# A gated mix of an S4 convolution and linear attention: the issue order written out instead of planned at build time

## The chip, the cores and the metric

The kernel runs on one core of a Trainium2 chip. It uses five engines, each of which works through its own queue of instructions in order: TensorE (PE; its weight loads are listed apart as PEld), VectorE (DVE), ScalarE (ACT), GpSimd (POOL) and SyncE (SP), which issues nearly all DMAs. The metric is the device time of one launch in microseconds, the median of several runs.

## The reference

The inputs are u of shape [1, 2048, 512] in bf16, the parameters of a state space model (128 states for each of 512 channels), the weights of a linear attention with 32 heads of 16, and a gate vector. The output mixes two branches that read the same u:

```python
x = A_u
g = _sigmoid((x * gate_w).sum(-1, keepdims=True))
a = _A_ref(x, A_A_re, A_A_im, A_B_re, A_B_im, A_C_re, A_C_im, A_log_dt, A_Dskip)
b = _B_ref(x, B_wqkv, B_w_phi, B_wo)
return g * a + (1 - g) * b
```

Branch a builds a kernel K of length 2048 for each channel and convolves u with it by an FFT of length 4096; it then adds u times Dskip:

```python
logdA = dt * A
dB = dt * Bc
P = jnp.exp(logdA[:, :, None] * l[None, None, :])
K = jnp.einsum("dn,dnl,dn->dl", Cc, P, dB).real
...
Yf = Uf * Kf[None, :, :, :]
```

Branch b applies a softmax of the projection and one of its negative to queries and keys, and normalises:

```python
phi_q = jnp.concatenate([_softmax(pq, axis=-1), _softmax(-pq, axis=-1)], axis=-1)
phi_k = jnp.concatenate([_softmax(pk, axis=-1), _softmax(-pk, axis=-1)], axis=-1)
kv = jnp.einsum("bhsf,bhsd->bhfd", phi_k, v)
z  = jnp.einsum("bhsf->bhf", phi_k)
num = jnp.einsum("bhqf,bhfd->bhqd", phi_q, kv)
den = jnp.einsum("bhqf,bhf->bhq", phi_q, z)[..., None] + 1e-6
```

num / den goes through the output projection wo.

## The kernel before

The whole program is recorded before any instruction is issued. The class `Plan` (L92) holds 1009 nodes. A node is a short piece of work of one engine: a group of matmuls into one PSUM tile, one activation, one or a few VectorE operations, a few DMA issues. `add` (L112) gives it an engine, a cost estimate, the nodes that it depends on, and the buffers that it takes and drops. `run` issues the nodes one after the other, and since each engine's queue is worked in order, the order of the nodes is the order on every engine. Waits between engines follow from the tiles that the nodes read and write.

Buffers come in rings: two each of Ek and vr (exponentials and scaled values of a key block), A and R (the factors of the convolution kernel), XA, XK and bs, four of E and cs, one of KD and XUs. PSUM has rings too: `ps` (2), `p0` (2, until the polar stage ends), `bk` (3 banks, for keys, values, queries, aexp and bps), and `pf` (2, in place of bk once the queries are done). `prepare` (L146) turns a full ring into a dependency: the third A waits for the reader of the first.

Before the change, `schedule` (L161) makes the order at build time. It simulates the engines with the cost estimates and a latency LAT of 0.2 between engines, and takes next, of the nodes that could start earliest, the one with the longest chain of work behind it; a table TIES of seeds and amplitudes adds random numbers to these priorities. It also decides for each of 53 PSUM evictions (`evict`, L650 ff.) whether ACT (L662) or DVE (L660) does it, and which PSUM ring a tile comes from.

The work goes through these stages, in order of time:

- Prologue: loads (L1423 to L1437; UD is u laid out for the FFT, sixteen DMAs), trigonometric tables by DVE (`tgv`, L397/L398) and ACT, their parts TB (L414) and TJ (L428), small constants of the attention (L302 to L329), transposes of u (xps, L595).
- Polar stage: the state space parameters in polar form (L455 to L590, from `dtc`, the step size), and the spectrum of u: psA (L681) and psB (L293) on PE, cast to XAu and XU by ACT or DVE.
- Keys: for eight pairs of blocks of 128 positions, pk (L803), exp to Ek (ACT), its sums Zk (DVE, L815), a logarithm and an exponential on ACT, values vp (L835), scaling to vr (DVE, L839) and the product kvp (L848).
- KV: the state is arranged (L919 to L931), multiplied with wo (mps, L955) and cast to Mw.
- Queries: four rounds of pq (L981), Eq = exp (ACT), sums zs (L996/L1000), lnZ, den and apm (L1012 to L1021), the factor aexp (L1041), Eq times aexp (DVE, L1046), the product bps (L1056) and its cast bs (ACT, L1066). Beside them runs the making of K: PE makes args (L876/L894), ACT takes exponentials E and sines and cosines cs; between the two kinds it loads another table (L75). DVE multiplies tables into A (three operations a half, L1102 to L1104) and E with cs into R (two operations, L1116/L1117, and a negation, L1114). PE contracts them (kps, L280, two chunks for each pair), ACT casts to KD (L1135), PE transforms (psA, L1147), ACT casts to XA (L1153).
- Convolution: the rest of the making of K, and psB (L1206), XK (ACT, L1214), t = XU times XK (DVE, L1221/L1222), psz (L1244), Zr, a round trip through memory (L1254, L1263), psy (L1301/L1307), the gated sum bS (DVE, L1328) and the stores (L1336).
- Tail: the last transforms and stores (L1276 to L1336).

Of the kernel before, what the change touches and what calls it, by code (L numbers as in the profile page):

```python
# [91 lines left out]
class Plan:  # L92


    LAT = 0.2
    SLACK = 0.0
    TIES = ((52116, 4, 0.1), (24065, 0.5, 0.1), (41416, 1, 0.1), (45222, 1, 0.05), (61293, 2, 0.02), (71070, 0.5, 0.1),
# [48 lines left out]
    def prepare(self):  # L146
# [11 lines left out]
        for n in reversed(self.nodes):  # L158
            n.prio = n.cost + max([u.prio + self.LAT * (u.eng != n.eng) for u in n.users], default=0.0)

    def schedule(self, bias, slack=0.0):  # L161

        free, taken = {}, {r: 0 for r in self.k}
        given = {r: {} for r in self.k}
        shut, state, since, order = set(self.shut), None, {}, []
        for n in self.nodes:
            n.t, n.ring, n.open, n.ready = None, None, len(n.deps), 0.0
        left = [n for n in self.nodes if not n.open]
        while left:
            cand = []  # L170
            for n in left:
                best_e = None
                for e, c in (n.eng if isinstance(n.eng, list) else [(n.eng, n.cost)]):
                    t = free.get(e, 0.0) if e not in "WX" else 0.0
                    for d in n.deps:
                        x = d.end + (self.LAT if d.at != e else 0.0)
                        if x > t:
                            t = x
                    if best_e is None or t + c < best_e[0]:
                        best_e = (t + c, t, e, c)  # L180
                _, t, e, c = best_e
                if n.tab is not None and n.tab != state:
                    continue
                ok, ring = True, None
                for r in n.take:
                    if isinstance(r, str) and r not in self.dyn:
                        continue
                    alt = []
                    for q in ([r] if isinstance(r, str) else r):
                        m = taken[q] - self.k[q]  # L190
                        if q in shut or (m >= 0 and m not in given[q]):
                            continue
                        alt.append((max(t, given[q][m].end + self.LAT if m >= 0 else since[q].end if q in since else 0.0), -self.k[q] + taken[q], q))
# [1365 lines left out]
```

## Time and profile before

| | before |
|---|---|
| median of 3 runs | 340.84 us (338.55 to 341.11) |
| span of the profiled execution | 340.1 us |
| mean granted TensorE clock | 0.836 |
| DVE busy | 279.3 us (82%), 478 instructions |
| ACT busy | 257.2 us (76%), 332 instructions |
| PE busy | 249.9 us (73%), 4320 matmuls |
| POOL busy | 12.2 us |
| DMA | 24.6 MB, 72 GB/s over the span |

The profile is of one execution, whose span is that of the first to the last instruction. A view by windows gives each engine's busy time in a stretch of the span; a view of waits gives, by engine and line, how long it stood idle and whose result ended that. Matmuls are pipelined, so a busy PE is not one at its peak.

### The profile page before, as it was taken

The numbers are of one execution on the slowest core, as the hardware profiler recorded it, in microseconds if no ns is written. First come the engines' busy times: TensorE is split into PE (matmuls) and PEld (weight loads), VectorE is DVE, ScalarE is ACT, GpSimd is POOL, SyncE is SP. The second block draws the span as 40 slices with busy tenths as digits, with TensorE's granted clock in tenths as the row PEclk, the third lists the DMA queues.
The fourth block names the chain that finished last, engine by engine and source line by source line (L and its number), as shares of the span: only waits on it lengthen the run. The fifth ranks groups of instructions, "written<-read, shape, count | busy, mean of one in ns | idle before, by whom it ended". The sixth has DMA issues, their size and how long they took to land.

```text
span 340.1 us, 9815 instructions
## 1 busy us (share of the span) xinstructions
PE 249.9 (73%) x4320; PEld 145.7 (43%) x4320; DVE 279.3 (82%) x478; ACT 257.2 (76%) x332; POOL 12.2 (4%) x24
## 2 busy tenths in 40 slices
PE   0416665469998979569999998976776769878860
PEld 0405554355554424233644544534343433456630
DVE  8968999995897985997598896399999999994531
ACT  2847998896978557965976897899979998888200
POOL 5420010000000000000000000000000000000000
PEclk9956569576999978957999999996997995797775
DMA  9991600000000000001111011281177178768444
GB/s 138 253 152 34 153 3 0 2 0 2 2 3 2 4 0 2 2 1 29 37 24 26 17 33 31 48 222 45 64 185 148 60 179 192 187 174 173 113 77 81
DMA packets 58665, 24.62 MB, mean 72 GB/s; under 512 B 54144, under 2 KB 55296, under 8 KB 58112
## 3 DMA queue, kind: packets, MB, share of 16 engines
q1 hardware_dynamic: 54400, 23.10, 31.1%
q10 hardware_dynamic: 4224, 0.92, 1.9%
q8 instruction: 33, 0.54, 0.7%
q14 instruction: 8, 0.07, 0.1%
HBM read 11.42 MB, written 8.39 MB: 58 GB/s over the span
## 4 chain that ended last, share of the span: by engine, by line
DVE 40%; PE 37%; ACT 7%; issue 6%; DMA 4%; SPq 3%; ACTq 1%; DVEq 0%
PE bps L1056 7%; DVE R L1117 5%; DVE A L1104 5%; DVE Atmp L1103 5%; DVE A L1102 5%; PE pk L803 5%; PE vp L835 4%; PE pq L981 3%; PE args L876 3%; SPq L1428 3%; DVE R L1116 3%; DMA Cim<-in_A_C_im_dram 2%; PE kps L280 2%; PE aexp L1041 2%; PE psz L1276 2%
## 5 line engine op out<-in xcount | busy, mean ns | idle before, releaser
L83 ACT ACTIVATE E<-args 128x1024 bf16<-128x1024 f32 x32 | 32.1, 1039 | 3.7 <-PE args L876 3.6
L1056 PE MATMUL bps<-Mw,Eq 128*128 128x512 bf16 x128 | 31.9, 394 | 1.1 <-DVE Eq L1046 1.1
L83 ACT ACTIVATE cs<-args 128x1024 bf16<-128x1024 f32 x32 | 30.8, 1034 | 0.1
L1046 DVE TENSOR_TENSOR Eq<-Eq,aexp 128x512 bf16<-128x512 bf16 x32 | 20.4, 682 | 10.2 <-PE aexp L1041 10.2
L681 PE MATMUL psA<-W,UD 128*64 128x256 bf16 x128 | 15.6, 396 | 16.8 <-DMA ldc<-in_A_log_dt_dram 5.7
L75 ACT ACT_TABLE_LOAD x20 | 25.7, 1283 | 1.1 <-PEq L1543 0.7
L1116 DVE TENSOR_TENSOR R<-E,cs 128x1024 bf16<-128x1024 bf16 x32 | 21.9, 685 | 4.4 <-PE kps L280 4.4
L876 PE MATMUL args<-selE,stat 64*128 64x512 bf16 x64 | 21.3, 446 | 5.1 <-ACT cs L83 2.9
L280 PE MATMUL kps<-R,A 128*32 128x64 bf16 x1024 | 18.9, 230 | 8.2 <-DVE A L1104 3.8
L815 DVE TENSOR_REDUCE Zk<-Ek 128x64 f32<-128x1024 bf16 x16 | 18.8, 1214 | 6.0 <-ACT Ek L83 5.8
L1104 DVE TENSOR_TENSOR A<-A,Atmp 128x1024 bf16<-128x1024 bf16 x32 | 22.1, 692 | 1.1
L1102 DVE TENSOR_TENSOR A<-Ctab,Dtab 128x1024 bf16<-128x1024 bf16 x32 | 21.9, 685 | 1.2 <-PE kps L280 1.2
L83 ACT ACTIVATE Ek<-pk 128x512 bf16<-128x512 f32 x32 | 16.7, 603 | 7.9 <-PE pk L803 7.9
L280 PEld LDWEIGHTS <-A 128*32 128x32 bf16 x1024 | 17.2, 152 | 12.0 <-issue 7.1
L1103 DVE TENSOR_TENSOR Atmp<-Ctab,Dtab 128x1024 bf16<-128x1024 bf16 x32 | 21.9, 684 | 0.0
L595 PE MATMUL xps<-ident,UD 128*128 128x128 bf16 x64 | 7.5, 296 | 18.9 <-DVE tgv L397 10.4
L1244 PE MATMUL psz<-t,TI 128*128 128x512 bf16 x56 | 18.2, 457 | 4.2 <-ACT cs L83 3.0
L681 PEld LDWEIGHTS <-UD 128*64 128x64 bf16 x128 | 12.2, 205 | 20.1 <-issue 19.8
L839 DVE TENSOR_TENSOR vr<-vp,vr 128x512 bf16<-128x512 f32 x32 | 19.6, 682 | 0.0
L83 ACT ACTIVATE Eq<-pq 128x512 bf16<-128x512 f32 x32 | 16.8, 614 | 3.3 <-PE pq L981 3.3
L1056 PEld LDWEIGHTS <-Eq 128*128 128x128 bf16 x128 | 12.0, 101 | 16.9 <-DVE Eq L1046 3.0
L1214 ACT CAST XK<-psB 128x1024 bf16<-128x1024 f32 x16 | 16.1, 1027 | 1.5 <-PE psB L1206 1.0
(195 smaller groups left out, 564.4 us busy)
## 6 DMA issues: line engine op xcount, KB each, us to landing
XUs<-XU SPq DMA_DIRECT2D x8, 512.0 KB, 6.6
Zd<-Zr SPq DMA_DIRECT2D x14, 256.0 KB, 4.8
ZT<-Zd SPq DMA_DIRECT2D x6, 512.0 KB, 5.5
UD<-in_A_u_dram SPq DMA_DIRECT2D x16, 128.0 KB, 5.4
bSd<-bs SPq DMA_DIRECT2D x16, 128.0 KB, 1.9
bS<-bSd SPq DMA_DIRECT2D x4, 512.0 KB, 7.9
out_dram<-bS SPq DMA_DIRECT2D x30, 64.0 KB, 2.3
wqk<-in_B_wqkv_dram SPq DMA_DIRECT2D x1, 1024.0 KB, 6.4
```

The lines of the kernel that those rows point to most:

```text
L75: p = self.nc.scalar.preload_act_table_set(name)
L83: i = self.nc.scalar.activation(**kw)
L280: nc.tensor.matmul(kps[32 * dj:32 * dj + 32, g4, e, :], lhsT=A[:, ri, :, :, d].rearrange("p a b -> p (a b)"), rhs=R[:, ri, d, :], start=(r ...
L681: nc.tensor.matmul(box.ps[64 * e:64 * e + 64, i, :], lhsT=g.UD[:].rearrange("p t (e g) -> p g e t", e=2)[:, gw * h + 4 * g4 + i, e, :], rh ...
L839: nc.vector.tensor_tensor(out=K.v[:, u, sg, :, 0:32].rearrange("p m (h e) -> p m h e", e=16), in0=box.ps[:].rearrange("p (m h e) -> p m h ...
L876: nc.tensor.matmul(box.ps[:, 8 * j:8 * j + 8, :], lhsT=g.stat[0:64, G, :], rhs=g.selE[0:64, d0:d0 + 8, :], start=True, stop=True, tile_pos ...
L1046: nc.vector.tensor_tensor(out=e, in0=e, in1=box.ps[:], op=ALU.mult)
L1056: nc.tensor.matmul(box.ps[:], lhsT=Q.e[:, m, sg, 128 * i:128 * i + 128], rhs=g.Mw[:, 4 * sg + m, :], start=(k == 0), stop=False, skip_grou ...
L1102: nc.vector.tensor_tensor(out=c.A[:, o], in0=Cb(i0), in1=Db(j0), op=ALU.mult)
L1103: nc.vector.tensor_tensor(out=tmp[:], in0=Cb(i1), in1=Db(j1), op=ALU.mult)
L1104: nc.vector.tensor_tensor(out=c.A[:, o], in0=c.A[:, o], in1=tmp[:], op=op)
L1116: nc.vector.tensor_tensor(out=c.R[:, o, :, 32:64], in0=E[:, :, 32:64], in1=x, op=ALU.mult)
```

## The change

The planner is gone. The class holds a string ORDER with the 1009 node numbers in the order in which they are issued, two digits to the base 64 each; SIDES, one digit for each of the 53 evictions (0 is ACT, 1 is DVE); and RINGS, one for each PSUM tile that has a choice of rings. `run` asserts that every node comes after those it depends on. Nodes, tiles, rings and operations are those of before; 15 evictions go to DVE and 38 to ACT, as before, but not all the same ones. The tables tell a reader nothing and are cut.

```diff
-    LAT = 0.2
-    SLACK = 0.0
-    TIES = ((52116, 4, 0.1), (24065, 0.5, 0.1), (41416, 1, 0.1), (45222, 1, 0.05), (61293, 2, 0.02), (71070, 0.5, 0.1),
...
+    DIGITS = "0123456789abcdefghijklmnopqrstuvwxyzABCDEFGHIJKLMNOPQRSTUVWXYZ-_"
+    ORDER = ("000f0g0h0b0c2u01040C0k0y0l0m0D0E0z0i0A0B0907050d02060F0a2o0n0j0p0q0e0r0t0u2v0o0G0s0v2s082p030H2t2q2r2k2l0w0I0J2F2G0K0M"
...
+    SIDES = ("00000000001010101000101010000000100100010011000010110")
...
-        for n in reversed(self.nodes):
-            n.prio = n.cost + max([u.prio + self.LAT * (u.eng != n.eng) for u in n.users], default=0.0)
-
-    def schedule(self, bias, slack=0.0):
...
-    def run(self):
-        self.tail = {}
+    def run(self):
+        code = {d: i for i, d in enumerate(self.DIGITS)}
+        order = [64 * code[a] + code[b] for a, b in zip(self.ORDER[0::2], self.ORDER[1::2])]
+        assert sorted(order) == list(range(len(self.nodes)))
+        names, sides, rings = [r for r in self.k if r in self.dyn], iter(self.SIDES), iter(self.RINGS)
+        for n in self.nodes:
+            n.at = n.eng[int(next(sides))][0] if isinstance(n.eng, list) else n.eng
+            n.ring = names[int(next(rings))] if n.dyn else None
         self.prepare()
-        T, order = self.schedule(self.bias(self.TIES), self.SLACK)
-        assert order is not None, "no piece can start"
-        for n in order:
+        done = set()
+        for i in order:
+            n = self.nodes[i]
+            assert all(d.i in done for d in n.deps)
+            done.add(i)
             self.cur = n
             n.fn()
-        return T
```

Three places show what moves. Lines of the new kernel are 70 lower than the same lines before (L590 is L660, L976 is L1046).

The first is DVE in the prologue. Before (tgv are the arguments of the trigonometric tables, TB and TJ two of these tables, the last row is the first of the attention's constants):

```order
L397 TENSOR_SCALAR tgv_161<-tgc,one 128x1024
L398 TENSOR_SCALAR tgv_161<-tgv_161 128x1024
L414 TENSOR_SCALAR TB<-TB 128x32x64
L397 TENSOR_SCALAR tgv_162<-tgc,one 128x1024
L398 TENSOR_SCALAR tgv_162<-tgv_162 128x1024
L428 TENSOR_SCALAR TJ<-tj 128x1024
L302 TENSOR_SCALAR mask_295<-c_293,if_h_140 128x8
```

And after (XAu is the cast of psA, the first stage of u's spectrum; pt is the first operation of the polar stage):

```order
L327 TENSOR_SCALAR tgv_157<-tgc,one 128x1024
L328 TENSOR_SCALAR tgv_157<-tgv_157 128x1024
L590 CAST XAu<-psA 128x256x4
L327 TENSOR_SCALAR tgv_158<-tgc,one 128x1024
L328 TENSOR_SCALAR tgv_158<-tgv_158 128x1024
L358 TENSOR_SCALAR TJ<-tj 128x1024
L344 TENSOR_SCALAR TB<-TB 128x32x64
L358 TENSOR_SCALAR TJ<-tj 128x1024
L590 CAST XAu<-psA 128x256x4 x2
L385 SCALAR_TENSOR_TENSOR pt_355<-Are,dtc 128x512
```

A cast of psA has come between the two pairs of trigonometric steps, and two more ahead of the polar stage; the attention's constants have moved behind it. On SP, the sixteen loads of UD, which psA reads, stand together in the new order; before, the five loads of weights (wc, gw, Dcol_b, wqk, Wv) stood between the first four and the other twelve.

The second place is ACT from the last key block to the first queries. Before (Zk and vr end a key block, Eq is the exponential of a query, Mw the attention's state with wo, cs the sines and cosines, E the exponentials, lnZ opens a query round):

```order
L83 ACTIVATE Zk<-Zk 128x128
L83 ACTIVATE vr<-Zk 128x64x2
L83 ACTIVATE E<-args 128x1024 x4
L83 ACTIVATE Eq<-pq 128x512 x14
L662 CAST Mw<-mps 128x1024
L83 ACTIVATE Eq<-pq 128x512 x2
L662 CAST Mw<-mps 128x1024
L75 ACT_TABLE_LOAD
L83 ACTIVATE cs<-args 128x1024 x4
L75 ACT_TABLE_LOAD
L83 ACTIVATE lnZ<-zs 128x256
```

And after:

```order
L83 ACTIVATE Zk<-Zk 128x128
L83 ACTIVATE vr<-Zk 128x64x2
L75 ACT_TABLE_LOAD
L83 ACTIVATE cs<-args 128x1024 x4
L75 ACT_TABLE_LOAD
L83 ACTIVATE Eq<-pq 128x512 x4
L592 CAST Mw<-mps 128x1024
L83 ACTIVATE Eq<-pq 128x512 x2
L592 CAST Mw<-mps 128x1024
L83 ACTIVATE Eq<-pq 128x512 x2
L83 ACTIVATE lnZ<-zs 128x256
```

The block of two table loads and four cs now stands right behind the last key block, and no longer between the last Mw and lnZ; some of the Eq stand ahead of these rows, others behind lnZ.

The third place is DVE at the end of the queries. Before (den, lnZ and Eq belong to the last query round, A, R and ns to the making of K):

```order
L1021 TENSOR_TENSOR lnZ<-lnZ,den 128x256
L1046 TENSOR_TENSOR Eq<-Eq,aexp 128x4x128 x8
L1116 TENSOR_TENSOR R<-E,cs 128x32x32
L1117 TENSOR_TENSOR R<-E,cs 128x32x32
L1114 TENSOR_SCALAR ns<-cs 128x1024
L1116 TENSOR_TENSOR R<-E,cs 128x32x32
L1117 TENSOR_TENSOR R<-E,ns 128x32x32
```

And after:

```order
L951 TENSOR_TENSOR lnZ<-lnZ,den 128x256
L976 TENSOR_TENSOR Eq<-Eq,aexp 128x4x128 x3
L1032 TENSOR_TENSOR A<-Ctab,Dtab 128x1024
L1033 TENSOR_TENSOR Atmp<-Ctab,Dtab 128x1024
L1034 TENSOR_TENSOR A<-A,Atmp 128x1024
L976 TENSOR_TENSOR Eq<-Eq,aexp 128x4x128 x2
L1046 TENSOR_TENSOR R<-E,cs 128x32x32
L1047 TENSOR_TENSOR R<-E,cs 128x32x32
L1032 TENSOR_TENSOR A<-Ctab,Dtab 128x1024
L1033 TENSOR_TENSOR Atmp<-Ctab,Dtab 128x1024
L1034 TENSOR_TENSOR A<-A,Atmp 128x1024
L976 TENSOR_TENSOR Eq<-Eq,aexp 128x4x128 x4
```

Two halves of an A and one of an R now stand between the last multiplies of Eq with aexp, which before stood in one row of eight.

More of the change, by code (lines that the diff above doesn't have):

```diff
@@ L107, in __init__ @@
+    SIDES = ("00000000001010101000101010000000100100010011000010110")
+    RINGS = ("1101100101000111101101010011011000000000000000000000022222222222222222222222222222222000002222222222222222222222222222"
+             "2222222222222222222222222222222222220000000000000000000000000000003300333030030000000330000000300033030030330033033303"
+             "303033030030030333333030333300")
     def __init__(self, rings, psum):
@@ L237, in bias @@
-    def bias(self, seeds):
-        import random
-        b = [0.0] * len(self.nodes)
-        for s, amp, share in seeds:
-            r = random.Random(s)
-            for i in range(len(b)):
-                if r.random() < share:
-                    b[i] += r.uniform(-amp, amp)
-        return b
-    def run(self):
-        self.tail = {}
-        self.prepare()
-        T, order = self.schedule(self.bias(self.TIES), self.SLACK)
-        assert order is not None, "no piece can start"
-        for n in order:
+    def run(self):
[3 more added lines that the diff above has]
+        names, sides, rings = [r for r in self.k if r in self.dyn], iter(self.SIDES), iter(self.RINGS)
+        for n in self.nodes:
+            n.at = n.eng[int(next(sides))][0] if isinstance(n.eng, list) else n.eng
+            n.ring = names[int(next(rings))] if n.dyn else None
+        self.prepare()
+        done = set()
[3 more added lines that the diff above has]
+            done.add(i)
```

89 lines of the change are left out of this document (17 added, 72 removed), and 8 rows, old and new, of the table TIES.

## The prediction

> **What bounds the kernel now.** I read the busy time of the engines by stage first, then what VectorE (DVE) waited for, then the rows around the waits. One median run takes 340.84 us; the profiled execution has a span of 340.1 us, so I add 0.7 us to a span to get a time. The windows view, cut where the work changes (columns: length, busy time of PE, PEld, DVE, ACT, POOL with instruction counts, granted PE clock, DMA share, GB/s):
>
> ```profile
> core 0: us, PE busy (x) PEld busy (x) DVE busy (x) ACT busy (x) POOL busy (x), PEclk, DMA share, GB/s
> 0.00:16.05 16.05, 3.95 (x40) 3.81 (x40) 14.05 (x41) 8.14 (x9) 7.74 (x16) 1.00 1.10 197
> 16.05:26.20 10.15, 1.23 (x10) 1.02 (x12) 6.45 (x20) 4.71 (x6) 3.25 (x6) 0.55 1.23 144
> 26.20:76.60 50.40, 30.74 (x392) 25.67 (x390) 49.23 (x80) 46.51 (x57) 1.24 (x3) 0.67 0.14 32
> 76.60:81.50 4.90, 4.90 (x45) 2.77 (x43) 1.74 (x4) 2.77 (x5) 0.00 (x0) 0.50 0.01 3
> 81.50:126.30 44.80, 41.73 (x690) 20.60 (x688) 40.95 (x52) 31.71 (x59) 0.00 (x0) 0.96 0.01 2
> 126.30:153.80 27.50, 20.66 (x261) 9.53 (x260) 21.39 (x43) 22.98 (x36) 0.00 (x0) 0.75 0.01 1
> 153.80:219.70 65.90, 64.18 (x681) 31.58 (x683) 49.90 (x88) 51.35 (x73) 0.00 (x0) 0.98 0.14 30
> 219.70:223.70 4.00, 3.15 (x133) 2.33 (x133) 2.77 (x6) 3.97 (x5) 0.00 (x0) 1.00 0.54 117
> 223.70:311.00 87.30, 64.30 (x1433) 37.14 (x1432) 84.42 (x138) 79.89 (x83) 0.00 (x0) 0.84 0.60 149
> 311.00:340.10 29.10, 15.07 (x654) 11.24 (x652) 8.44 (x9) 5.14 (x6) 0.00 (x0) 0.73 0.46 94
> sum 340.10, PE 249.91 PEld 145.69 DVE 279.33 ACT 257.17 POOL 12.23; mean PE 24.99 PEld 14.57 DVE 27.93 ACT 25.72 POOL 1.22
> ```
>
> The stages are the prologue (two windows), the polar stage (26.2 to 76.6), a junction, the keys (81.5 to 126.3), the way from the last key to the first product bps (126.3 to 153.8), the queries (to 219.7), a second junction, the convolution (to 311) and the tail. DVE is the busiest engine. Length minus its busy time gives its idle time, window by window: 2.0, 3.7, 1.2, 3.2, 3.9, 6.1, 16.0, 1.2, 2.9, 20.7; in all 60.8 us. In the queries PE is nearly full (64.2 of 65.9) and DVE waits for it; in the polar stage and the convolution DVE is full. The longest DVE waits, from the view of waits (total, times, longest):
>
> ```profile
> DVE Eq L1046 <- PE aexp L1041: 10.2, 6, 3.7
> DVE Zk L815 <- ACT Ek L83: 5.8, 5, 2.2
> DVE t L1221 <- ACT XK L1214: 5.3, 3, 4.1
> DVE Z L1285 <- PE psz L1276: 5.2, 1, 5.2
> DVE R L1116 <- PE kps L280: 4.4, 1, 4.4
> DVE pt L455 <- ACT dtc L83: 3.3, 1, 3.3
> ```
>
> **The change, part by part.** No operation is added or removed and as many evictions stay on DVE, so DVE's 279.3 us stay, and the span is 279.3 us plus DVE's idle time. I walked the new sequences of the four engines by hand with the durations of the trace and compare idle time, stage by stage.
>
> *Prologue, +2.3 us.* The rows of the SP queue and the first psA product, from the timeline (start, duration, engine):
>
> ```profile
> 6.17 0.41 SPq L1433 DMA_DIRECT2D wc<-in_B_w_phi_dram  x1
> ...
> 11.18 9.73 SPq L1428 DMA_DIRECT2D UD<-in_A_u_dram  x12
> 25.98 1.12 PE L681 MATMUL psA<-W,UD 128*64 128x256 bf16 x8 [5.66 <-DMA ldc<-in_A_log_dt_dram]
> ```
>
> All loads of UD now go ahead of the five weight loads, so the last twelve start 11.18 − 6.17 = 5.0 us earlier, and psA, which needs them all, at 26.0 − 5.0 = 21.0. But a psA cast now stands in DVE's queue right behind the work that ended at 16.05. It can start at 21.0 + 1.1 = 22.1; behind it wait the second pair of trig steps, TJ and the negation of TB. So DVE idles 6.0 us there; the 3.3 us wait for dtc goes, since more work stands ahead of it. Idle goes from 5.7 to 2.0 + 6.0 = 8.0. If UD landed no earlier than now, the idle would be 5 us more (+7.3); if the loads were not slowed at all by what shares the queue, the cast would hardly wait (0). I take 2.3 because the shift of 5.0 is a row of this queue.
>
> *Polar stage, +1.5 us.* Six casts of XU leave the keys for this stage. The rows by group (busy us, mean ns):
>
> ```profile
> L662 ACT CAST XU<-psB 128x1024 bf16<-128x1024 f32 x12 | 11.7, 1014 | 1.3 <-PE psB L293 1.3
> ...
> L75 ACT ACT_TABLE_LOAD x20 | 25.7, 1283 | 1.1 <-PEq L1543 0.7
> L1104 DVE TENSOR_TENSOR A<-A,Atmp 128x1024 bf16<-128x1024 bf16 x32 | 22.1, 692 | 1.1
> L1102 DVE TENSOR_TENSOR A<-Ctab,Dtab 128x1024 bf16<-128x1024 bf16 x32 | 21.9, 685 | 1.2 <-PE kps L280 1.2
> L1116 DVE TENSOR_TENSOR R<-E,cs 128x1024 bf16<-128x1024 bf16 x32 | 21.9, 685 | 4.4 <-PE kps L280 4.4
> L1103 DVE TENSOR_TENSOR Atmp<-Ctab,Dtab 128x1024 bf16<-128x1024 bf16 x32 | 21.9, 684 | 0.0
> L876 PE MATMUL args<-selE,stat 64*128 64x512 bf16 x64 | 21.3, 446 | 5.1 <-ACT cs L83 2.9 <-ACT E L83 1.0 <-ACT KD L1135 0.8
> ...
> L280 PE MATMUL kps<-R,A 128*32 128x64 bf16 x1024 | 18.9, 230 | 8.2 <-DVE A L1104 3.8 <-ACT cs L83 2.7 <-issue 0.9
> ...
> L981 PE MATMUL pq<-xT,Wqp 128*128 128x512 bf16 x64 | 16.7, 398 | 0.0
> ```
>
> Six times 1.01 is 6.1 us of ACT, in a stage where ACT has 50.4 − 46.5 = 3.9 us free. DVE feels it only where it needs a result of ACT, and it has casts of its own to do in between: bounds 0 and +6, and I take 1.5, near the low end, because DVE waited only 1.2 us there although ACT was 92% busy.
>
> *Junction, −2.2, and keys, −2.9 us.* DVE idles 3.2 us before the first key sum; now three casts stand there (Wkp and two XU, 1 us and more each), leaving about 1.0. In the keys the six XU casts are gone from ACT, on which the waits of 5.8 us for Ek fell, and selE's construction fills one of those waits; 3.9 becomes about 1.0. Three query products now share the banks of the key products, so bounds are 0 and −3.9.
>
> *End of keys to end of queries, −11.5 us.* This is the main term. Now, between the last key scaling and the first bps, ACT runs this block (timeline, ACT alone):
>
> ```profile
> 139.43 1.28 ACT L75 ACT_TABLE_LOAD   x1
> 140.72 3.77 ACT L83 ACTIVATE cs<-args 128x1024 bf16<-128x1024 f32 x4
> 144.51 1.28 ACT L75 ACT_TABLE_LOAD   x1
> 145.81 0.38 ACT L83 ACTIVATE lnZ<-zs 128x256 f32<-128x256 f32 x1
> ```
>
> That is 145.81 − 139.43 = 6.4 us ahead of the first lnZ, on which aexp, the Eq multiply and bps hang. The new order runs the block before the last queries' exponentials, while PE still has keys to do, and the last key product no longer stands behind a query product. By my walk the first bps comes 18.5 us after the last scaling instead of 27.5. What is that worth? PE idles 27.5 − 20.7 = 6.8 us ahead of the first bps, and I leave it 2.0, so 4.8 go. PE also gets two kernel chunks (2 × 18.9/16 = 2.4) and three args pairs net (3 × 21.3/32 = 2.0), and gives up three pq products (3 × 16.7/16 = 3.1): net 1.3. So the last bps can come x = 4.8 − 1.3 = 3.5 us earlier, with no PE idle at all 7.3. Second, one A half, another, and one R half (2 × 3 × 0.69 + 2 × 0.69 = 5.5 us) now stand between the last Eq multiplies, in DVE's waits for aexp. Third, the wait of 4.4 us for kps goes, as kps now comes ahead of the last four bps. Of DVE's 23.3 us idle (6.1 + 16.0 + 1.2), x + 5.5 + 4.4 = 13.4 would go, at most 17.2. An A half waits until kps has read its buffer, and behind it in DVE's queue stand the Eq multiplies and, for them, bps. Whether each A half is free in time I can't see; I leave out 2 us and take 11.5. If none finds it, 3.5 + 4.4 = 7.9 are left; if the block is still late, 4.4.
>
> A rule that speaks against this stands beside a row. From the chain of waits:
>
> ```profile
> 153.88 3.42 PE bps L1056 x8
> 157.53 1.73 PE bps L1056 x8
> ```
>
> The first product after PE had been mostly idle took twice the later ones: 1.7 us more. The Trainium skill, "TensorE: Matmul & The Clock Gate", section "Part 1: The HAM clock gate", says that the array drops to half rate after an idle window of about 3.4 us and needs as long of work to return; by that rule every new pause of PE would cost such a doubled product. The trace agrees here, and its 0.98 in the queries says that no pause was that long. With two such pauses the sum would be 3.4 us worse, which is inside the range.
>
> *Convolution, +1.6 us.* Of ACT's 79.9 us, one KD, four E and two cos or sin, each on a tile of 128x1024 as the XU cast (7 × 1.01), and two table loads (2 × 1.28) have gone ahead, 9.6 us. But DVE, at 84.4 of 87.3, has less left to hide its remaining waits (5.3 us for XK), and stages hand one another A and R through two buffers each. I take 2.9 → 4.5, bounds −2 and +8.
>
> *Tail, 0.* It begins when the last t is done, and its 29.1 us hang on DMA round trips that the order does not shorten. psy products are swapped, but the last stores still queue behind one another; bounds ±2.
>
> Sum: 2.3 + 1.5 − 2.2 − 2.9 − 11.5 + 1.6 = −11.2. Span 340.1 − 11.2 = 328.9, time **329.6 us**.
>
> **Rivals.**
>
> *A: the idle time moves to the convolution.* What the queries give, the convolution takes back: A and R done early only means that DVE meets full rings (two buffers each), XK and the XUs loads sooner. For it: the waits of 5.3 us for XK with ACT at 79.9 of 87.3. Against it: ACT gets lighter by 9.6 us. Priced at 8 us instead of 1.6 it gives −4.8, 336 us; with the polar bound too (+4.5) 340.5.
>
> *B: slower, bs held up behind table blocks.* ACT empties bps by the cast bs. Now the four cs of a block always stood in twos with a bs between, once bps had begun; in the new order two blocks stand whole ahead of a bs: load, four cs and the second load, 1.28 + 3.77 + 1.28 = 6.3 us. bps, aexp and pq share three banks, so PE can stop. Fully uncovered, two blocks cost 12.6, and PE's half rate afterwards 2 × 1.7: the sum becomes −11.2 + 16.0 = +4.8, time 345.6. It decides from 3.9 us uncovered per block, with the half rate (2 × 3.9 + 3.4 = 11.2). For it: PE is at 64.2 of 65.9, so all it loses shows. Against it: DVE's A and R work and args for PE stand in the gap, and in my walk the first block meets PE while only one product is out. The Trainium skill, in the section "Architectural detail: the array is 16× 32×32, not 1× 128×128" of the page named above, calls ACT and DVE strict FIFO, which is what makes this possible; every wait above shows in queue order, so the trace agrees.
>
> *C: better than forecast.* UD lands soon enough for the prologue cast (−2.3), the polar stage hides its casts (−1.5), and the queries give 15 (−3.5): −18.5, 322.3 us.
>
> *That nothing moves* is out: on the engines named, instructions stand in other places.
>
> **How the numbers follow.** Forecast 0.56 (its own range 324 to 335), A 0.22, C 0.13, B 0.09. The range of 320 to 339.5 leaves out B and the worst end of A, some 0.14, and a little below. About 1% is what a measurement here tells from no change, since the three runs spread by 0.8%; that is 337.4 to 344.2. A lies half above 337.4: faster 0.56 + 0.13 + 0.10 = 0.79, less 0.02 for the upper end of the forecast; same 0.13; slower 0.10, B and a hundredth of A in which the prologue's bound (+5) comes on top.
>
> **What would show it.** In the new trace: the first psA ends near 22 and DVE idles about 6 us from 16; the first bps comes about 18 us after the last scaling; no wait of R for kps at the end of the queries; DVE idle from the end of keys to the start of the convolution near 12 instead of 23.3; DVE's total idle near 50. Rival A shows as more than 8 us of DVE idle in the convolution, with waits for XK, kps or XUs; rival B as PE idle in the queries before a bps, released by ACT bs. The forecast fails if the first bps stays over 24 us behind the last scaling, or if psA still starts at 26.

## The result and the profile after

The new order takes 325.5 us (median of 4 runs, 324.0 to 331.0); the kernel before takes 339.7 beside it. The ratio is 0.958, 95% interval 0.951 to 0.965. The profiled execution has a span of 324.5 us and a mean granted clock of 0.863, where before it was 340.1 us and 0.836. A run measures 1.8 us more than its span, not the 0.7 that the prediction added. Ratios and their intervals leave out executions more than 1.5% longer than the shortest of the same kernel, medians and ranges do not; two profiles among the experiments (the convolution of before, and the R wait) are of such executions, and from these only the stages that their edits touch are compared, and the clock in the queries.

The windows view of the new kernel, cut at the same places of the program as the one of before (prologue in one window, convolution with the second junction):

```profile
core 0: us, PE busy (x) PEld busy (x) DVE busy (x) ACT busy (x) POOL busy (x), PEclk, DMA share, GB/s
0.00:27.25 27.25, 11.24 (x112) 9.99 (x113) 20.60 (x49) 17.61 (x20) 9.41 (x21) 0.94 1.05 170
27.25:75.35 48.10, 28.61 (x440) 23.44 (x440) 46.19 (x92) 47.05 (x59) 1.25 (x3) 0.64 0.15 34
75.35:79.50 4.15, 3.84 (x28) 2.02 (x25) 3.80 (x5) 2.58 (x5) 0.00 (x0) 0.60 0.00 0
79.50:121.30 41.80, 40.84 (x668) 18.24 (x675) 40.52 (x51) 35.26 (x66) 0.00 (x0) 1.00 0.01 2
121.30:138.90 17.60, 14.55 (x179) 6.91 (x181) 16.02 (x36) 16.59 (x25) 0.00 (x0) 0.94 0.01 2
138.90:208.30 69.40, 67.41 (x810) 33.95 (x814) 63.83 (x112) 59.47 (x83) 0.00 (x0) 0.97 0.13 29
208.30:293.80 85.50, 60.00 (x1414) 35.57 (x1426) 79.37 (x129) 73.22 (x76) 0.00 (x0) 0.84 0.61 156
293.80:324.50 30.70, 13.38 (x652) 10.10 (x651) 8.44 (x9) 5.18 (x6) 0.00 (x0) 0.78 0.46 93
```

DVE's idle time is length minus its busy time. It falls from 60.8 to 45.7 us, and its busy time from 279.3 to 278.8; together that is the 15.6 us of span.

| stage | DVE idle before | after | change | forecast |
|---|---|---|---|---|
| prologue | 5.7 | 6.7 | +1.0 | +2.3 |
| polar stage | 1.2 | 1.9 | +0.7 | +1.5 |
| junction | 3.2 | 0.4 | −2.8 | −2.2 |
| keys | 3.9 | 1.3 | −2.6 | −2.9 |
| last key to last bps, with the wait at the seam | 23.3 | 7.2 | −16.1 | −11.5 |
| convolution | 2.9 | 6.1 | +3.2 | +1.6 |
| tail | 20.7 | 22.3 | +1.6 | 0 |

Before, the wait of R for kps runs 1.2 us past the last bps; the table counts this with the queries, as the prediction does, and the convolution of before begins behind it.

DVE's longest waits in the new kernel, from the view of waits (total, times, longest):

```profile
DVE Z L1215 <- PE psz L1206: 5.0, 1, 5.0
DVE t L1151 <- ACT XK L1144: 4.5, 2, 4.0
DVE XAu L590 <- PE psA L611: 3.9, 1, 3.9
DVE Eq L976 <- PE aexp L971: 3.4, 6, 1.3
DVE bS L1260 <- PE psy L1249: 3.1, 1, 3.1
DVE R L1046 <- ACT XA L1083: 2.2, 1, 2.2
DVE A L1032 <- PE kps L210: 2.0, 1, 2.0
```

The wait of Eq for aexp has gone from 10.2 to 3.4 us, that of Zk for Ek (5.8) and the one of 4.4 us of R from the list; new are the cast of psA in the prologue and, in the convolution, an R that waits 2.2 us and an A that waits 2.0 us. The view puts that R down to the cast XA, which ended 0.01 us before it. The kps that still reads its buffer ended 0.13 us before it. At the R that waits for kps in the R-wait kernel below the distance is 0.12 us, so the text takes it for a wait for this buffer.

### The profile page after: what moved, and what is told of

Same layout as the page of the kernel before. It is cut to its first block, busy times and chain, and to the rows that moved or that the text cites. A ratio compares the mean times of both kernels' runs of the same rounds, so it can differ in the third digit from the quotient of the medians.

```text
span 324.5 us, 9787 instructions
## 1 busy us (share of the span) xinstructions
PE 239.9 (74%) x4289; PEld 140.2 (43%) x4320; DVE 278.8 (86%) x478; ACT 257.0 (79%) x332; POOL 10.7 (3%) x24
## 4 chain that ended last, share of the span: by engine, by line
PE 36%; DVE 27%; ACT 21%; issue 7%; DMA 4%; SPq 2%; ACTq 0%; DVEq 0%
PE bps L986 7%; PE pk L733 4%; PE kps L210 4%; PE vp L765 3%; ACT L75 3%; PE args L806 3%; DVE Atmp L1033 2%; DVE A L1032 2%; SPq L1358 2%; DVE A L1034 2%; DVE R L1046 2%; DVE R L1047 2%; PE psA L1077 2%; PE pq L911 2%; ACT E L83 2%
## 5 line engine op out<-in xcount | busy, mean ns | idle before, releaser
L986 PE MATMUL bps<-Mw,Eq 128*128 128x512 bf16 x122 | 30.4, 383 | 1.0 <-DVE Eq L976 0.5
L1174 PE MATMUL psz<-t,TI 128*128 128x512 bf16 x46 | 17.5, 456 | 8.7 <-DVE t L1151 3.0
L1046 DVE TENSOR_TENSOR R<-E,cs 128x1024 bf16<-128x1024 bf16 x32 | 21.9, 683 | 2.2 <-ACT XA L1083 2.2
L976 DVE TENSOR_TENSOR Eq<-Eq,aexp 128x512 bf16<-128x512 bf16 x32 | 20.7, 681 | 3.5 <-PE aexp L971 3.4
L611 PE MATMUL psA<-W,UD 128*64 128x256 bf16 x128 | 14.3, 373 | 12.0 <-ACT XAu L592 6.3
L806 PE MATMUL args<-selE,stat 64*128 64x512 bf16 x64 | 19.8, 401 | 2.8 <-ACT E L83 2.6
L223 PE MATMUL psB<-XAu,TB 64*128 64x128 bf16 x256 | 12.6, 262 | 7.6 <-DVE XU L590 3.9
L611 PEld LDWEIGHTS <-UD 128*64 128x64 bf16 x128 | 11.5, 202 | 14.3 <-issue 11.1
```

The source lines that it names most:

```text
L611: nc.tensor.matmul(box.ps[64 * e:64 * e + 64, i, :], lhsT=g.UD[:].rearrange("p t (e g) -> p g e t", e=2)[:, gw * h + 4 * g4 + i, e, :], rh ...
L806: nc.tensor.matmul(box.ps[:, 8 * j:8 * j + 8, :], lhsT=g.stat[0:64, G, :], rhs=g.selE[0:64, d0:d0 + 8, :], start=True, stop=True, tile_pos ...
L976: nc.vector.tensor_tensor(out=e, in0=e, in1=box.ps[:], op=ALU.mult)
L986: nc.tensor.matmul(box.ps[:], lhsT=Q.e[:, m, sg, 128 * i:128 * i + 128], rhs=g.Mw[:, 4 * sg + m, :], start=(k == 0), stop=False, skip_grou ...
L1046: nc.vector.tensor_tensor(out=c.R[:, o, :, 32:64], in0=E[:, :, 32:64], in1=x, op=ALU.mult)
```

## The experiments

Each kernel is the new one with some of the issue order put otherwise; the work is the same in all. Each length "last key to first bps" runs from the end of the last vr scaling on DVE to the start of the first bps on PE, and is 27.5 us before and 17.6 after.

### Which part of the order brings the gain: front and back apart

```diff
  order up to and with the last kvp:
-   the new one
+   that of before
  order behind it: the new one
```

> Everything up to the last key product in the order of before, the rest in the new order. Theory (as predicted: the stages add up, and the query gain comes from the place of the table block): the front stages lose what they gained, DVE idle +3.7 us by the two traces (0.95 + 0.74 - 2.81 - 2.57 the other way), and the query stage keeps its gain: about 329 us. Rival (ACT load: what the front did was to clear ACT's queue, by doing query exponentials and E tiles during the keys): with the old front these stand in the way again between the last key and the first lnZ, about 7 us more: about 336 us, and the first bps over 22 us behind the last key scaling instead of 17.5.

Measured: 341.5 us, ratio to before 1.007 (1.002 to 1.012). Nothing of the gain is left. Its way from the last key to the first bps, by windows:

```profile
125.50:153.20 27.70, 19.54 (x263) 8.51 (x266) 14.60 (x33) 24.61 (x36) 0.00 (x0) 0.93 0.01 1
```

It is as long as before, and ACT is busy for 24.6 of 27.7 us, where the new kernel has 16.6 of 17.6. So the rival holds, and more strongly than it was put (336 us): not only is ACT's queue full, but the queries behind then take 70 us, as in the new kernel, instead of 66, since the new order puts more of the making of K into them.

```diff
  order up to and with the last kvp: the new one
  order behind it:
-   the new one
+   that of before
```

> The new order up to the last key product, the order of before behind it. The reverse, the old front with the new order behind, took as long as before. Theory (each part alone is worth its own stages): the front stages keep 3.7 us of idle, 335 to 337 us. Rival (the new front only frees ACT for what the new order puts there; the old order doesn't use it): 338 to 341 us. If the front alone gave most of the gain: under 331 us.

Measured: ratio 0.984 (0.979 to 0.990), 333.9 us, 6 us less than before. The keys end at 122.6 instead of 126.3, which is the 3.7 us of the front stages, and the way to the first bps is 2 us shorter:

```profile
122.60:148.10 25.50, 14.43 (x175) 6.96 (x175) 22.00 (x45) 14.23 (x24) 0.00 (x0) 0.75 0.01 2
```

ACT is now busy for only 14.2 us of it. The old order does not use that: in DVE's queue it has 8.5 us of A and R operations ahead of den, and ACT waits 8.2 us for that den:

```profile
142.54 0.40 ACT L83 ACTIVATE den<-den,eps 128x128 f32<-128x128 f32 x1 [8.24 <-DVE den L943]
```

The kernel before has the same operations ahead of den, without a gap (timeline of DVE):

```profile
138.87 0.68 DVE L1102 TENSOR_TENSOR A<-Ctab,Dtab 128x1024 bf16<-128x1024 bf16 x1
...
147.40 0.42 DVE L1012 TENSOR_TENSOR den<-zs,den 128x256 f32<-128x256 f32 x1
```

There the first lnZ came at 145.8, so that den on DVE was late by under 1 us; it would have stood in the way as soon as ACT was ready sooner. In the new kernel 2.0 us of such work stand ahead of den (one A half, from 129.84). No run puts DVE's part back by itself. The 333.9 us lie between the expectations: less than 335 to 337, and more than the 331 at which the front would have most of the gain.

The back alone gives nothing, the front alone 6 us, both 14 us: more than half of the gain exists only with both.

### Between the last key and the first bps

The prediction put its main term on the place of the block of two table loads and four cs. In the new kernel ACT has this sequence (timeline of ACT: start, duration):

```profile
118.34 0.32 ACT L83 ACTIVATE vr<-Zk 128x128 bf16<-128x128 f32 x1
118.67 1.28 ACT L75 ACT_TABLE_LOAD   x1
119.97 3.77 ACT L83 ACTIVATE cs<-args 128x1024 bf16<-128x1024 f32 x4
123.76 1.28 ACT L75 ACT_TABLE_LOAD   x1
125.05 2.06 ACT L83 ACTIVATE Eq<-pq 128x512 bf16<-128x512 f32 x4
126.98 1.04 ACT L592 CAST Mw<-mps 128x1024 bf16<-128x1024 f32 x1
...
131.23 0.40 ACT L83 ACTIVATE lnZ<-zs 128x256 f32<-128x256 f32 x1
```

ACT does not stop between the last key block and the first Mw. The block alone was put back (rows of ACT):

```diff
 L83 ACTIVATE vr<-Zk 128x64x2
-L75 ACT_TABLE_LOAD
-L83 ACTIVATE cs<-args 128x1024 x4
-L75 ACT_TABLE_LOAD
 L83 ACTIVATE Eq<-pq 128x512 x4
...
 L83 ACTIVATE Eq<-pq 128x512 x2
+L75 ACT_TABLE_LOAD
+L83 ACTIVATE cs<-args 128x1024 x4
+L75 ACT_TABLE_LOAD
 L83 ACTIVATE lnZ<-zs 128x256
```

> The new order, but the block of two table loads and four cs stands again right before the first lnZ, behind the exponentials of the queries, with its args. Theory (the block's place makes the gain, as predicted): the first lnZ and the first bps come 6.4 us later, time about 330 us. Rival (ACT load): the block only fills the time in which ACT would wait for the first query product behind the last key, 118.7 to about 122.6 in the new trace, so 3.9 us are lost at most, and 2 us or less if ACT has other work: 326 to 329 us.

Measured: ratio 0.991 (0.986 to 0.995), 337.5 us; the way to the first bps is 25.8 us, 8.2 more than in the new kernel. Both expectations were too small. Its ACT sequence shows why:

```profile
118.31 0.31 ACT L83 ACTIVATE vr<-Zk 128x128 bf16<-128x128 f32 x1
122.61 1.08 ACT L83 ACTIVATE Eq<-pq 128x512 bf16<-128x512 f32 x2 [3.99 <-PE pq L911]
124.33 1.09 ACT L83 ACTIVATE Eq<-pq 128x512 bf16<-128x512 f32 x2 [0.64 <-PE pq L911]
126.83 1.01 ACT L592 CAST Mw<-mps 128x1024 bf16<-128x1024 f32 x1 [1.41 <-PE mps L885]
...
131.98 1.09 ACT L83 ACTIVATE Eq<-pq 128x512 bf16<-128x512 f32 x2 [1.65 <-PE args L824]
133.07 1.28 ACT L75 ACT_TABLE_LOAD   x1
134.36 3.77 ACT L83 ACTIVATE cs<-args 128x1024 bf16<-128x1024 f32 x4
138.15 1.28 ACT L75 ACT_TABLE_LOAD   x1
139.44 0.38 ACT L83 ACTIVATE lnZ<-zs 128x256 f32<-128x256 f32 x1
```

Where the block stood, ACT now waits 4.0 us for the first query product; behind, it waits for products and for args that stand ahead in PE's queue; and then the block comes on top. lnZ is at 139.4 instead of 131.2. The block in its new place is free: it fills time in which ACT has nothing else. The 8.2 us agree with the profiled span, which is 7.9 us longer than the new kernel's (332.4 against 324.5). The median lies 3.3 us above this execution (334.2), and no profile shows what the longer ones lose.

Then the three query products that the new order does among the keys were put behind them again, with the block in its new place:

```diff
  among the keys (PE; ACT):
-   pq, Eq x2; pq, Eq x2; pq, Eq x2
  behind the last kvp and the block:
+   pq, Eq x2; pq, Eq x2; pq, Eq x2
    pq, Eq x2
```

> The new order with the block in its new place, but the three query products that were done among the keys, and their six exponentials, stand behind the last key product again. Theory (the block's place makes the gain): no change beyond 1 us in the first bps, 325 us. Rival (ACT load): ACT gets six exponentials of 0.6 us, 3.7 us, between the block and the first lnZ, and PE three products of 1.0 us: first bps 3 to 4 us later, time 328 to 330 us.

Measured: 333.4 us (329.3 to 334.4, 4 runs), ratio 0.980 (0.971 to 0.989). The way to the first bps:

```profile
121.80:143.40 21.60, 16.84 (x190) 7.84 (x192) 15.47 (x35) 19.04 (x31) 0.00 (x0) 0.97 0.01 2
```

It is 4.0 us longer, as the rival said: ACT's busy time on it grows by 2.5 and its idle time by 1.6. So the early products are a part of the gain of their own. The time is longer by more than this, 7.9 us: in the profile (span 332.1) the queries took 73.2 us instead of 69.5 with PE longer at half rate, which the last section of the experiments takes up.

Both together:

> The new order with both steps undone between the last key and the first bps: the block stands before the first lnZ and the three query products with their six exponentials stand behind the last key. Singly they cost 8.4 and 4.1 us on that way (17.5 us in the new kernel). Theory (ACT's work on that way sets its length; what is put back adds up): 17.5 + 6.3 + 3.7 of work and some waiting for PE, 29 to 31 us, time 336 to 339 us. Rival (the two hide one another, ACT doing the six exponentials while it would wait for PE): 25 to 27 us, not more than with the block alone, 332 to 336 us.

Measured: ratio 0.997 (0.993 to 1.001), 337.8 us.

```profile
120.60:150.50 29.90, 21.95 (x193) 9.24 (x195) 15.94 (x36) 22.69 (x33) 0.00 (x0) 0.79 0.01 1
```

29.9 us: 17.6 + 8.2 + 4.0 = 29.8. On this way the two add up, as the theory had it. Of the 12.3 us more, ACT works for 6.1 and stands idle for 6.2, waiting for products of PE, so it is the order in the queues of both and not ACT's work alone. The times do not add up (12.0 and 7.9 us singly, 12.3 together), since each single one also holds what is said of it above. With both undone the new order is worth what before is. Its DVE idle time is 57.7 us, 12 us more than in the new kernel, all of it on this way.

### The work put between the last Eq multiplies

```diff
-L976 TENSOR_TENSOR Eq<-Eq,aexp 128x4x128 x3
-L1032 TENSOR_TENSOR A<-Ctab,Dtab 128x1024
...
-L976 TENSOR_TENSOR Eq<-Eq,aexp 128x4x128 x4
+L976 TENSOR_TENSOR Eq<-Eq,aexp 128x4x128 x9
+L1032 TENSOR_TENSOR A<-Ctab,Dtab 128x1024
...
```

> The new order, but the two halves of an A and the half of an R that stand between the last Eq multiplies are moved behind the last of them. Theory (they fill DVE's waits for aexp, as predicted): DVE idles 5.3 us more in the queries and all that follows is later by that, less the 2.2 us in which DVE waits for a buffer of R at the start of the convolution: 3 to 5 us slower than the new order, 328 to 330 us. Rival (PE sets the pace there and the A halves would find room later): no change, 324 to 326 us.

Measured: 328.5 us (326.2 to 330.7, 4 runs), ratio 0.967 (0.960 to 0.974), which overlaps the new kernel's; the profiled span is 324.4 us, the new kernel's 324.5. The windows of this kernel for queries and convolution (to the last R):

```profile
139.00:208.20 69.20, 67.16 (x810) 33.99 (x814) 58.91 (x103) 59.48 (x83) 0.00 (x0) 0.97 0.13 29
208.20:288.60 80.40, 54.95 (x1290) 32.25 (x1301) 79.46 (x133) 70.60 (x73) 0.00 (x0) 0.84 0.60 155
```

and for the convolution of the new kernel:

```profile
208.30:288.60 80.30, 55.02 (x1299) 32.03 (x1313) 74.67 (x124) 70.68 (x73) 0.00 (x0) 0.86 0.59 155
```

DVE idles 10.3 us in the queries instead of 5.6, and 0.9 us in the convolution instead of 5.6. Both stages keep their lengths. The A and R halves done early only bring DVE sooner to the buffers that are not yet free, the two waits of 2.2 and 2.0 us above among them. So the rival holds in the profiles. The runs don't exclude the theory: two are at 326.2 and 326.6, two at 330.5 and 330.7, the median lies in its range, and no profile shows a longer one.

### The convolution

```diff
  order up to and with the last bps: the new one
  order behind it:
-   the new one
+   that of before
```

> New order up to the last bps, then the order of before for the convolution and the tail. In the new trace convolution and tail have 3.6 us more DVE idle than before (2.0 + 1.6). Theory 1 (rival A of the prediction, in small: idle time moves there because the queries end earlier and the rings are full): the old order would not help, 324 to 327 us. Theory 2 (it is the new order of these stages itself): about 321 to 322 us, with the waits of R for its buffer (2.2 us) and of A for kps (2.0 us) gone.

Measured: 326.2 us (321.4 to 328.9), ratio 0.954 (0.944 to 0.964). The time lies in the range of theory 1. In the trace the wait of R and that of A are gone, as theory 2 has it, but a t now waits for the load of XUs, which can be issued only when the queries are done:

```profile
221.84 0.69 DVE L1152 TENSOR_TENSOR t<-XUs,XK 128x1024 bf16<-128x1024 bf16 x1 [3.38 <-DMA XUs<-XU]
```

Also an exponential stood ahead of the table load meant for it and got one of its own. These two were mended: psA, kps and one pair of A and R ahead of the first t, the exponential behind its table load, and bS loaded after the first Zd.

```diff
 L1034 TENSOR_TENSOR A<-A,Atmp 128x1024
-L1151 TENSOR_TENSOR t<-XU,XK 128x1024
-L1152 TENSOR_TENSOR t<-XUs,XK 128x1024
...
 L1047 TENSOR_TENSOR R<-E,cs 128x32x32
+L1151 TENSOR_TENSOR t<-XU,XK 128x1024
+L1152 TENSOR_TENSOR t<-XUs,XK 128x1024
```

> As the run with the convolution and tail of before behind the new front and queries, with two stalls of its trace taken away: the first t waited 3.4 us for the load of XUs, so psA, kps and one pair of A and R come ahead of it and the two loads of bS behind; and an exponential stood ahead of the table load meant for it, which cost a load of its own. Theory (the order of the convolution is worth what its waits show): 3 us less DVE idle in the convolution than in that run, 4 to 6 us less than the new order in convolution and tail together: 319 to 322 us. Rival (the end hangs on PE, ACT and DMA in the tail, so what DVE gains waits there): 323 to 326 us.

Measured: 322.3 us (320.9 to 326.0, 6 runs), ratio 0.949 (0.943 to 0.954). Its convolution, to the last R, and what follows:

```profile
208.20:284.20 76.00, 55.34 (x1283) 32.80 (x1287) 74.57 (x124) 68.28 (x72) 0.00 (x0) 0.87 0.65 164
284.20:319.90 35.70, 19.70 (x790) 14.71 (x788) 13.27 (x15) 9.62 (x10) 0.00 (x0) 0.72 0.52 106
```

76.0 us with 1.4 idle, against 80.3 with 5.6; what follows the last R takes 35.7 against 35.9. So 4.3 us of length were in the new order of the convolution and not in what the earlier stages hand it. The time is a little above the theory's 319 to 322 and below the rival's. The A and R halves stand early here too, and the convolution behind them no longer idles; so that they are worth nothing is shown for the new convolution only, and no run takes them out of this kernel. This is the shortest kernel of the study, 3.2 us under the changed one by the medians, though the two intervals meet (0.951 to 0.965 and 0.943 to 0.954); with that of the second measurement of the changed kernel (0.955 to 0.965, below) it does not.

A single one of those waits was also tried by itself, with the rest of the new order untouched:

```diff
  PE behind the last bps:
-   args x3, psA x2, kps
+   psA x2, kps, args x3
```

> The new order, but at the start of the convolution psA of the fourth pair and the first kps behind it stand ahead of the args products, one of which waits 2.2 us for an exponential in the new trace; R waits 2.2 us for this kps there. Theory (a wait of the fullest engine is worth its length): the wait of R goes, DVE idle in the convolution falls from 5.6 to 3.5 us, and the time by 2 us against the unaltered kernel beside it. Rival (the wait comes back later, at A for kps or at t for XK): DVE idle in the convolution stays at 5 to 6 us, no change.

Measured: 330.3 us (326.5 to 332.2, 6 runs), ratio 0.971 (0.964 to 0.977): no shorter than the unaltered kernel, whose ratio beside it was 0.960 (0.955 to 0.965), and rather longer. The wait was not removed but moved to a later R:

```profile
DVE R L1046 <- PE kps L210: 3.1, 1, 3.1
```

DVE idle in the convolution was 7.2 us. The rival held, with more idle time than it was put at. The edit also moved two casts XA on ACT ahead of three exponentials E, and the first of them waited, with the E behind it:

```profile
216.49 1.93 ACT L1083 CAST XA<-psA 128x1024 bf16<-128x1024 f32 x2 [2.69 <-DMA bSd<-bs]
```

On PE the args that went back, on which later E and R hang, stand ahead of the later kps. Which of the two made that kps late was not tried apart.

### Prologue, clock, and the changed kernel again

To the mended kernel one step was added, in which DVE does two table parts while it waits for psA:

```diff
 L328 TENSOR_SCALAR tgv_157<-tgv_157 128x1024
+L344 TENSOR_SCALAR TB<-TB 128x32x64
+L358 TENSOR_SCALAR TJ<-tj 128x1024
 L590 CAST XAu<-psA 128x256x4
```

> The mended convolution of the earlier run, with one change in the prologue: tj goes ahead of the second TB on ACT, so that DVE does the first TJ and the negation of TB while it waits for psA. DVE waited 3.9 us there; 1.1 us of work is put into it. Theory: prologue 1 us shorter, 319 to 322 us, 3 to 5 us less than the unaltered kernel. Rival (the second TB, now 1.1 us later, holds up the second pair of trigonometric steps by as much): as the earlier run, 321 to 323 us.

Measured: 323.0 us (320.3 to 326.0), ratio 0.952 (0.946 to 0.958). The prologue is 26.7 us instead of 27.5 in the mended kernel, but the whole is no shorter than without it, within what can be measured: inconclusive.

The changed kernel was run again beside these:

> The changed kernel itself, unaltered, as the standard for the three beside it and to see its spread. If the clock at the first kernel chunks decides between two lengths of the query stage (69.5 and 73.2 us in profiles so far, of kernels whose queries have the same order), its own times spread over some 4 us, 322 to 331, with the longer ones at the lower mean clock; if the difference came from the other kernels' changes, its times lie together and every profile of it shows 69 to 70 us.

Measured: 325.7 us (323.9 to 330.2, 6 runs), ratio 0.960 (0.955 to 0.965), as the first time. The spread of 2% came with the same kernel. Its order is that of the R-wait kernel up to the last bps, and yet its queries took 69.9 us in the profile and those of the other 73.8. The clock rows of both, around the first two kernel chunks kps; first the changed kernel, where kps begins at 146.26:

```profile
143.00:146.00 3.00, 1.71 (x8) 0.47 (x5) 2.97 (x6) 3.00 (x4) 0.00 (x0) 0.86 0.23 49
146.00:148.00 2.00, 2.00 (x120) 1.75 (x123) 1.93 (x6) 1.97 (x5) 0.00 (x0) 0.50 0.03 8
148.00:150.00 2.00, 1.86 (x32) 0.66 (x23) 2.00 (x5) 1.71 (x4) 0.00 (x0) 0.86 0.00 0
150.00:152.00 2.00, 1.74 (x10) 0.96 (x11) 2.00 (x5) 1.99 (x3) 0.00 (x0) 1.00 0.03 8
```

then the R-wait kernel, where it begins at 146.74:

```profile
144.00:147.00 3.00, 2.20 (x31) 1.06 (x31) 2.79 (x5) 2.97 (x5) 0.00 (x0) 1.00 0.20 44
147.00:148.00 1.00, 1.00 (x80) 1.00 (x77) 0.52 (x2) 1.00 (x2) 0.00 (x0) 0.80 0.07 16
148.00:156.00 8.00, 7.78 (x80) 3.11 (x73) 7.37 (x15) 7.02 (x9) 0.00 (x0) 0.50 0.01 2
156.00:158.00 2.00, 2.00 (x8) 0.78 (x6) 1.97 (x4) 0.58 (x1) 0.00 (x0) 0.54 0.10 24
```

In both PE pauses before the clock falls to half: 1.3 of 3.0 us in the one, 0.8 of 3.0 in the other. In the changed kernel it falls at 145.2, before kps begins (the 0.86 of the first row is 0.8 us at half rate), in the R-wait kernel at 147.6, in the middle of it. In the one it is back after 3.4 us, in the other only after 10.2, three times as long, with the first bps products at half rate, although PE was busy nearly all the time.

Eleven profiles are of kernels with this order on PE from the first bps to the last, and ten of them divide in this way. In seven (the changed kernel twice, the one with the block put back, both steps undone, the halves moved, and the two mended kernels) the fall came between 1.1 us before and 0.1 us after the start of kps; half rate lasted 3.4 us, and the queries took 69.2 to 69.9. In three (early products put back, the convolution of before, the R wait) it came 0.45 to 0.86 us after that start; half rate lasted 10.2 us, and the queries took 73.2 to 73.8. In the eleventh, behind the front of before, it came with the first bps, for 3.4 us, and the queries took 70.5. So the length of this stay at half rate goes with some 4 us of the queries; what makes it long is open.

To see whether the chunks' density sets it off, they were parted:

```diff
  PE:
-   args, kps, kps, args
+   kps, args, kps, args
```

> The new order, with the first two kernel chunks (kps, 64 narrow matmuls each) not one behind the other but with an args product between them, and one args product behind them. In two profiles with the same order of queries the clock fell to half at these chunks and stayed there for some 10 us, and the queries took 73.2 us instead of 69.5. If the density of narrow matmuls in a stretch of 3 us sets this off, the times lie nearer to the lower end (324 us) and the queries take 69 to 70 us in the profile; if it is chance or set off by something else, the times spread as those of the new order, 324 to 331 us.

Measured: 326.6 us (325.4 to 328.3, 6 runs), ratio 0.962 (0.958 to 0.967); the queries took 71.8 us in its profile. There the chunks ran at the full clock, and half rate came 2.6 us behind the second one, for 3.4 us. The times lie closer together than the changed kernel's, but not at its lower end: whether their density matters stays open.

## Why the prediction was right, and where it was not

The forecast was 329.6 us, the range 320 to 339.5; the time is 325.5. The mechanism was named in the right stage, and the sum of −11.2 was too small by 4.4 us of span (328.9 against 324.5). That it came so near is in part luck, since terms missed on both sides: the gain at the last bps was put 2.9 us too low, and 5.5 us of A and R halves were counted (less 2 of doubt) that gave no time. As 1.8 us lie outside the span and not 0.7, the profiled execution took 326.3 us, 3.3 under the forecast.

- **Prologue (+2.3).** Right in kind. The waiting cast of psA is there, but psA came at 19.7, not 21.0. The last load of UD is issued by 14.7 instead of 20.9, and psA starts 6.3 us earlier, not 5.0. The change is +1.0.

```profile
0.74 13.92 SPq L1358 DMA_DIRECT2D UD<-in_A_u_dram  x16
...
19.67 1.24 PE L611 MATMUL psA<-W,UD 128*64 128x256 bf16 x16 [2.56 <-DMA UD<-in_A_u_dram]
```

- **Polar stage, junction, keys (+1.5, −2.2, −2.9).** Measured are +0.7, −2.8 and −2.6. These were all near. What the step missed is what they were for: the front alone gives 6 us, but without it the back gives nothing. The prediction added the stages up as if each stood for itself.
- **Last key to last bps (−11.5).** The measured change is −16.1, and the parts of the step were weighed wrongly. *The first bps* was forecast at 18.5 us behind the last key and came at 17.6; undoing the block costs 8.2 of it and undoing the early query products 4.0. The prediction named the block, and booked the early products only as 3.1 us less for PE, not as exponentials off ACT's queue. For this way it reckoned with ACT alone and left out the 8.5 us of A and R operations ahead of den on DVE, which had to move too, as the front alone shows.

  *The last bps* could come x = 3.5 us earlier by the forecast, with 7.3 as a bound; behind the last key it came 93.4 − 87.0 = 6.4 earlier. PE's idle time on this stretch fell by 3.5 (8.6 to 5.0), less than the 4.8 reckoned. The rest is PE's busy time: it was to grow by 1.3 and fell by 2.9 (84.8 to 82.0), with 989 matmuls in place of 942, as PE spends less of it at half rate (clock 0.94 instead of 0.75 ahead of the first bps). The prediction had no term for that.

  *The A and R halves* (5.5 us) were the term that failed: DVE does idle less in the queries by them, but the convolution gives the time back, as the kernel with the halves moved shows with a span 0.1 us apart. That is what rival A says, for this term. *The R wait* (4.4 us) went as forecast; in the convolution 4.2 us of new waits for R and A stand against it, and no run shows it by itself.
- **Convolution (+1.6).** Mis-sized: +3.2, with 4.2 us of new waits for R and A. It is the order, not the early end of the queries: with the order of before, mended at two places, the convolution idles 1.4 us up to the last R, against 5.6. Most of the waits for XK that the prediction named here are not in this stage: of the 5.3 us before, 3.6 lie behind 311, in the tail, which does not begin when the last t is done, as the prediction says (t goes on to 317.1).
- **Tail (0).** +1.6 by the windows. From the last R to the end it is 35.0 us before, 35.9 after, and 35.2 in the second profile of the changed kernel. No run separates its cause.
- **Rival B** (bs behind table blocks) did not show: PE idles 2.0 of 69.4 us in the queries. **Rival A** did not by its own sign, more than 8 us of DVE idle in the convolution (6.1), and the mended convolution shows that most of this is the order there; only for the halves it is right. Of **rival C** the queries' part came (16.1 for 15), and its prologue and polar stage by about half (+1.0 and +0.7 instead of nothing).
- **The clock.** The prediction allowed for two doubled products, 3.4 us. The Trainium skill, "TensorE: Matmul & The Clock Gate", section "Part 1: The HAM clock gate", ties the half rate to an idle window. The rows here agree in part: PE paused before each fall shown, but for 1.3 and 0.8 us of 3.0, and half rate then also lasted 10.2 us with PE busy for 9.8 of 10.0. The same section calls the ramp run-variable; with 3.9 us between two profiles of one order of the queries, the trace agrees. The times of the repeated kernel follow their mean clocks only loosely (330.2 us at 0.862, but 323.9 at 0.865), so that the clock explains all of the spread is not shown; only one of these six executions was profiled.

## What to carry to other kernels

Where an order is changed as a whole, don't price its stages one by one: look for the engines that a stretch waits for at its start (here ACT between two stages, and DVE behind it), list what stands in their queues, and ask what an earlier stage must give up so that these queues are shorter. Work pulled into a waiting engine's gaps is worth its length only if the next stage needs it at once; here 5.5 us of it were given back by a convolution that had waits of its own, and a single wait of 2.2 us that was moved away came back elsewhere as 3.1. Filling a gap on the engine that sets the pace with work that has to be done anyway can be worth more than its own length: the table block was worth 8.2 us for 6.3, and its args on PE moved with it.

## What the runs showed of the hardware that was not expected

In the fourteen profiles every stay of the granted clock at 0.50 that ended before the kernel did lasted 3.4 us or a whole multiple of it, up to 37.5. It began behind stretches of 3.4 us in which PE was busy for 10 to 89%, so it needed no pause of that length. It did not end as soon as PE was busy: before the change it lasted from 75.1 to 81.9 with PE busy throughout, and at the first kps chunks 3.4 us in seven profiles and 10.2 in three, with queries of 69.2 to 69.9 and of 73.2 to 73.8 us. A kernel on one core, unaltered, spread from 323.9 to 330.2 us over six runs.
